# Mean and variance of h on ScalarE instead of VectorE, one iteration later

## The chip, the cores and the metric

The kernel runs on one core of a Trainium2 chip. A core has five engines with a queue each: TensorE (PE in the profile, its weight loads PEld), VectorE (DVE), ScalarE (ACT), GpSimd (POOL) and SyncE (SP), which here issues DMAs. The metric is the device time of one execution in microseconds.

## The reference

x is one sequence of 2048 tokens by 512 channels, in float32.

```python
x = A_x
h = x + A(layernorm(x))      # linear attention, 32 heads of 16
h2 = h + B(layernorm(h))     # token-mixing MLP, 2048 -> 1792 -> 2048
# A: q, k, v = x @ wqkv; phi = [softmax(p), softmax(-p)] of p = q @ w_phi (k likewise)
#    o = phi_q (phi_k^T v) / (phi_q . sum phi_k + 1e-6);  o @ wo
# B: layernorm again, u = gelu(h^T w1 + b1), y = (u w2 + b2)^T
```

`_layernorm` subtracts the mean over the 512 channels and divides by sqrt(variance + 1e-5). B applies it twice in a row, so the kernel computes one rstd that stands for both: (var·(1 + eps) + eps²)^(−1/2).

## The kernel before

Tokens lie on partitions, 16 tiles of 128 tokens. Matmuls in float32 are done as three passes over operands that are split in two parts: ScalarE rounds a value (`split`, line 56), and VectorE or GpSimd subtracts the rounded part from it (line 57).

The first stage (to about 146 us in the trace) makes keys, values and the attention state, and the queries of the first tiles. The last stage (from about 280 us) applies the rest of W1, the gelu and W2. Between them is the fused loop, `for it in range(NT + 3)`, in which the change lies. Each tile passes through it over several iterations. In iteration `it`:

- `s_num(it-1)`: TensorE makes the numerator in the PSUM tile `tn` (L544), ScalarE copies it rounded to `oh` (L548). `s_ol` later has VectorE subtract `oh` from `tn` into `ol` (L553).
- `s_wo(it-2)`: TensorE multiplies by wo into `po` (L61 to L63).
- `s_tr(it)`: TensorE transposes the scaled feature maps into `tn` (L526), ScalarE copies them to `pht` (L528). `tn` has one buffer, so the transposes wait until `ol` has read it.
- `lead(it)`: on GpSimd `s_pq(it+1)` multiplies a tile's 128x1024 feature map by its factors w (L452, called pq in the text) and `s_ez(it+3)` multiplies another by zB (L434), then the negation of logits (L159); on TensorE and ScalarE the query projections and exponentials that are still to do.
- `s_den(it+2)` and `q_sums`, `q_logits` on VectorE, ending in w (L449).
- `s_hn(it-3)`: ScalarE normalizes h into `hn` (L583) and rounds it to `hs` (L56), GpSimd subtracts for the low part of `hs` (L57).
- `s_h(it-2)`: VectorE adds `po` to x (L568), which gives h; SP writes it out; VectorE takes mean and variance (L571 to L575).
- `s_rstd(it-3)`, at the top of the iteration: GpSimd raises to the power −1/2 (L578) and multiplies the negated mean by it (L579).
- `fill`: TensorE accumulates the first two pairs of W1's column blocks with the tiles that are normalized already. `fill_load`, at the end of an iteration, brings 256 KB of W1, has ScalarE round it (`whi`, L56) and VectorE subtract (`wlo`, L57). By its condition, both pairs load at the ends of iterations 2, 6, 8, 10, 12, 14 and 16, and one pair each at the ends of 4 and 5.

The loop is written under `manual_schedule`, so TensorE, VectorE, ScalarE and GpSimd take its instructions in the order of the program. The last stage is ordered by the planner, which may place some of its instructions between the last ones of the loop; its first W2 load (L730) uses memory that the loop's last tiles occupy. In the trace, iteration n begins its copy `pht` at 147.23 (0), 155.65, 162.89, 170.30, 178.53, 187.04, 196.50, 204.36, 211.53 (8), 218.69, 225.84 (10), 232.99, and so on in steps of 7.15 to 261.61 (15).

Of the kernel before, what the change touches and what calls it, by code (L numbers as in the profile page):

```python
# [9 lines left out]
F32 = mybir.dt.float32  # L10
F32R = mybir.dt.float32r
AF = mybir.ActivationFunctionType
ALU = mybir.AluOpType
# [4 lines left out]
P = 128  # L18
S, D, H, DH, F = 2048, 512, 32, 16, 1792
NT = S // P  # L20
# [9 lines left out]
EPS = 1e-5  # L30
# [3 lines left out]
def block_kernel(ctx: ExitStack, tc: tile.TileContext, x, xT, wT, phic, wo, w1, b1, w2, b2,  # L34
                 kvmask, ident_in, out):
    nc = tc.nc

    cst = ctx.enter_context(tc.tile_pool(name="cst", bufs=1))
# [6 lines left out]
    b1s = cst.tile([P, NF], F32, name="b1s")  # L45
    b2s = cst.tile([P, NT], F32, name="b2s")
    r1 = cst.tile([P, NT], F32, name="r1")
    mv2 = cst.tile([P, NT, 2], F32, name="mv2")
    r2 = cst.tile([P, NT], F32, name="r2")
    cst.tile([P, 56], F32, name="pad")  # L50
    nc.vector.memset(ones, 1.0)
    nc.vector.memset(mhalf, -0.5)

    def split(hi, lo, src, lo_engine):

        nc.scalar.activation(hi, src, AF.Copy)  # L56
        lo_engine.tensor_sub(lo, src, hi)  # L57
# [97 lines left out]
    def negate():  # L155

        if MN:
            ev, mn = MN.pop(0)
            nc.gpsimd.tensor_sub(ev[:, :, 1], mn.unsqueeze(3).to_broadcast([P, NPR, 2, DH]), ev[:, :, 1])  # L159

    def run(*lists):

        for i in range(max(map(len, lists))):
            for ops in lists:
                if i < len(ops):
                    ops[i]()
# [4 lines left out]
    def heads(e):  # L171
        return e.rearrange("p g (a d) -> p (g a) d", d=DH)
# [186 lines left out]
    def q_mm():  # L359
        if q["mm"] < NT:  # L360
            PS[q["mm"]] = proj(q["mm"], wqh, wql, ps_q, "pu")
            q["mm"] += 1

    def q_logits(lag):
        n = q["logits"]
        if n < min(NT, q["mm"] - lag + NT * (q["mm"] == NT)):
            EQ[n] = big.tile([P, NG, P], F32, name="eq", tag="big")
            q["logits"] += 1
            return logit_ops(PS[n], EQ[n], n >= len(Q_AT))
        return []  # L370

    def q_exp(lag):
        n = q["exp"]
        if n < min(NT, q["logits"] - len(MN) - lag):
            exps(n, EQ[n])
            q["exp"] += 1

    def q_sums(lag):
        n = q["sum"]
        if n < min(NT, q["exp"] - lag + NT * (q["exp"] == NT)):  # L380
            q["sum"] += 1
            return q_sum(n)
        return []
# [48 lines left out]
    def s_ez(t):  # L432
        EZ[t] = az.tile([P, NG, P], F32, name="ez")
        nc.gpsimd.tensor_mul(EZ[t], EQ[t], zB)  # L434

    def s_den(t):


        tz = az.tile([P, NPR, 2, 2], F32, name="tz")
        den = az.tile([P, NPR, 2], F32, name="den")  # L440
        W[t] = az.tile([P, NPR, 2, 2], F32, name="w", bufs=3)
        other = SQ[t]
        return [lambda: nc.vector.reduce_sum(tz.rearrange("p g c h -> p (g c h)"), heads(EZ[t]), axis=AX.X),
                lambda: nc.vector.scalar_tensor_tensor(tz[:, :, 0], other[:, :, 1], 1e-6, tz[:, :, 0],
                                                       op0=ALU.mult, op1=ALU.add),
                lambda: nc.vector.tensor_mul(tz, other, tz),
                lambda: nc.vector.reduce_sum(den, tz.rearrange("p g c h -> p g h c"), axis=AX.X),
                lambda: nc.vector.reciprocal(den, den),
                lambda: nc.vector.tensor_mul(W[t], other, den.unsqueeze(2).to_broadcast([P, NPR, 2, 2]))]  # L449

    def s_pq(t):
        nc.gpsimd.tensor_mul(heads(EQ[t]), heads(EQ[t]), W[t].rearrange("p g c h -> p (g c h)").unsqueeze(2).to_broadcast([P, 2 * H, DH]))  # L452

    def lead(it, mm):

        if 0 <= it + 1 < NT:
            s_pq(it + 1)
        if 0 <= it + 3 < NT:
            s_ez(it + 3)
        negate()  # L460
        for _ in range(mm):
            q_mm()
        q_exp(0)
# [53 lines left out]
    ak = a2.enter_context(tc.tile_pool(name="ak", bufs=2, reuse_waits="tile"))  # L517
    ps_t = a2.enter_context(tc.tile_pool(name="ps_t", bufs=1, space=PSUM, reuse_waits="tile"))
    ps_o = a2.enter_context(tc.tile_pool(name="ps_o", bufs=1, space=PSUM, reuse_waits="tile"))
    HN, HT, PHT, OS, PO, VE = {}, {}, {}, {}, {}, {}  # L520

    def s_tr(t):
        PHT[t] = ak.tile([P, NG, P], F32, name="pht")
        ptr = ps_t.tile([P, 2, 4, P], F32, name="tn")
        for g in range(NG):
            nc.tensor.transpose(ptr[:, g // 4, g % 4, :], EQ[t][:, g, :], ident)  # L526
        for half in range(2):
            nc.scalar.activation(PHT[t][:, half * 4:half * 4 + 4, :], ptr[:, half], AF.Copy)  # L528

    def s_kv():  # L530

        pt = ps_o.tile([P, 2, P], F32, name="po")
        for b in range(2):
            nc.tensor.transpose(pt[:, b, :], kvS[:, 2 * b:2 * b + 2, :].rearrange("p n f -> p (n f)"), ident)
        nc.scalar.activation(kvB, pt, AF.Copy)

    def s_num(t):

        pn = ps_t.tile([P, 2, 4, P], F32, name="tn")[:, :, 0:2]
        for b in range(2):  # L540
            for c in range(4):
                for r in range(2):
                    rows, cols = slice(64 * r, 64 * r + 64), slice(32 * c, 32 * c + 32)
                    nc.tensor.matmul(pn[cols, r, b, :], kvB[rows, b, cols], PHT[t][rows, 4 * b + c, :],  # L544
                                     start=True, stop=True, skip_group_check=True)
        oh = ak.tile([P, 2, 2, P], F32R, name="oh")
        ol = ak.tile([P, 2, 2, P], F32R, name="ol")
        nc.scalar.activation(oh, pn, AF.Copy)  # L548
        OS[t] = oh, ol, pn

    def s_ol(t):
        oh, ol, pn = OS[t]
        return [lambda: nc.vector.tensor_sub(ol, pn, oh)]  # L553

    def s_wo(t):
        oh, ol, _ = OS.pop(t)
        PO[t] = po = ps_o.tile([P, D], F32, name="po")
        for j in range(4):
            mm3(po, oh[:, j // 2, j % 2, :], ol[:, j // 2, j % 2, :], woh[:, j, :], wol[:, j, :], j == 0, j == 3)

    def s_x(t):
        HT[t] = ak.tile([P, D], F32, name="h", bufs=4)
        nc.sync.dma_start(HT[t], x[t * P:(t + 1) * P, :])

    def s_h(t):

        h = HT[t]
        nc.vector.tensor_add(h, PO.pop(t), h)  # L568
        nc.sync.dma_start(out[t * P:(t + 1) * P, :], h)
        st = ak.tile([P, 6], F32, name="st2")  # L570
        nc.vector.bn_stats(st, h)  # L571
        nc.vector.bn_aggr(mv2[:, t, :], st)
        VE[t] = ak.tile([P, 2], F32, name="ve2")
        nc.vector.tensor_scalar(VE[t][:, 0:1], mv2[:, t, 1:2], 1.0 + EPS, EPS * EPS, op0=ALU.mult, op1=ALU.add)
        nc.vector.tensor_scalar_mul(VE[t][:, 1:2], mv2[:, t, 0:1], -1.0)  # L575

    def s_rstd(t):
        nc.gpsimd.tensor_tensor(r2[:, t:t + 1], VE[t][:, 0:1], mhalf[:, :1], op=ALU.pow)  # L578
        nc.gpsimd.tensor_mul(VE[t][:, 1:2], VE[t][:, 1:2], r2[:, t:t + 1])  # L579

    def s_hn(t):
        hn = ak.tile([P, D], F32, name="hn")
        nc.scalar.activation(hn, HT[t], AF.Identity, scale=r2[:, t:t + 1], bias=VE[t][:, 1:2])  # L583
        HN[t] = big.tile([P, 2, D], F32R, name="hs", tag="big")
        split(HN[t][:, 0], HN[t][:, 1], hn, nc.gpsimd)
# [34 lines left out]
    for it in range(NT + 3):  # L620
        if 0 <= it < NT:
            s_x(it)
        if 0 <= it - 3 < NT:
            s_rstd(it - 3)
        if 0 <= it - 1 < NT:
            s_num(it - 1)
        if 0 <= it - 2 < NT:
            s_wo(it - 2)
        if it == 1:
            q_mm()  # L630
        if 0 <= it < NT:
            s_tr(it)
        if it == 0:
            s_kv()
        lead(it, 1)
        den = s_den(it + 2) if it + 2 < NT else []
        run((s_ol(it - 1) if 0 <= it - 1 < NT else []) + q_logits(1) + (q_sums(0) if it > 0 else []), den)
        if it == 0:
            run(q_logits(0))
        if it > 0:  # L640
            negate()
        if 0 <= it - 3 < NT:
            s_hn(it - 3)
        if 0 <= it - 2 < NT:
            s_h(it - 2)
        if FN[0] <= it - LAG:
            fill(0, ps_f)
        for _ in range(2):
            if q["logits"] == NT and FN[1] <= it - LAG:
                fill(1, ps_q)  # L650
        for p in range(2):
            if it >= LAG - 2 and FL[p] <= FN[p] + 1:
                fill_load(p)
# [102 lines left out]
    for n, (sp, p) in enumerate(STEPS):  # L756
        t = 2 * sp
# [15 lines left out]
        if not last:  # L773
# [6 lines left out]
            for i, add in enumerate((u3.unsqueeze(1).to_broadcast([P, 2, HD]), e)):  # L780
                nc.vector.scalar_tensor_tensor(ot[:, i], bank[2 + i], b2s[:, t + i:t + i + 1], add,  # L781
                                               op0=ALU.add, op1=ALU.add)
# [68 lines left out]
```

## Time and profile before

| what | before |
|---|---|
| median of 3 runs | 540.12 us (540.0 to 540.82) |
| profiled execution's own time | 540.13 us |
| span of the profile | 538.3 us |
| PE busy | 526.6 us, 98% |
| DVE busy | 393.3 us, 73% |
| ACT busy | 257.9 us, 48% |
| POOL busy | 235.6 us, 44% |

The span runs from the first to the last instruction; the own time is a little longer. Shares are means over stages that differ. In a timeline row stand the start and the duration in us, the engine, the line of the kernel, the operation, what it writes and reads, the shapes, how many like instructions are merged, and in brackets the idle time of the engine before it and what ended that.

### The profile page before, as it was taken

To read this page: it belongs to the slowest core of one execution; us is meant where nothing else is said; L and a number is where in the kernel's file an instruction comes from. 1 tells how busy PE (TensorE), PEld (TensorE's weight loads), DVE (VectorE), ACT (ScalarE), POOL (GpSimd) and SP (SyncE) were. 2 spreads that over 40 slices of the span, in tenths; PEclk is the share of its full clock that TensorE was granted. 3 is DMA by queue.
4 is the path that set the end of the run, shared out by engine and by line. 5 is a ranking of instruction groups with operands and counts; after the bars stand their busy time and mean duration, and the time that the engine had idled before them with its cause. 6 is when DMAs were issued, how large, how long until landed. Compare 5 with 4: busy or idle time off the path is not lost.

```text
span 538.3 us, 9897 instructions
## 1 busy us (share of the span) xinstructions
PE 526.6 (98%) x3872; PEld 449.7 (84%) x3872; DVE 393.3 (73%) x722; ACT 257.9 (48%) x406; POOL 235.6 (44%) x184
## 2 busy tenths in 40 slices
PE   8999999999999999999999999999999999999995
PEld 7888778777776877787787888888899999999995
DVE  6992999974689989996447952224858878977784
ACT  6998733525346465444647433325552333343340
POOL 2589599788968979996432200000001101101110
PEclk9999999999999999999999999999999999999999
DMA  8633201012301233333254543333013565645631
GB/s 310 207 102 117 79 21 40 1 62 78 93 6 63 95 99 94 107 131 119 82 163 143 163 139 97 99 97 99 20 40 100 140 153 129 126 138 119 157 71 48
DMA packets 45486, 55.84 MB, mean 104 GB/s; under 512 B 3968, under 2 KB 33024, under 8 KB 45440
## 3 DMA queue, kind: packets, MB, share of 16 engines
q1 hardware_dynamic: 43136, 51.38, 30.1%
q0 software_dynamic: 2016, 3.67, 5.0%
q8 instruction: 30, 0.49, 0.4%
q10 hardware_dynamic: 288, 0.17, 0.1%
q14 instruction: 16, 0.13, 0.1%
HBM read 46.81 MB, written 8.39 MB: 103 GB/s over the span
## 4 chain that ended last, share of the span: by engine, by line
PE 85%; DVE 8%; ACT 2%; DMA 2%; issue 2%; POOL 0%; SPq 0%; DVEq 0%; POOLq 0%; ACTq 0%
PE py L745 26%; PE pu L61 10%; PE pu L63 10%; PE pu L62 10%; PE po L61 3%; PE pk_ps L61 3%; PE pv L62 3%; PE pv L61 3%; PE pv L63 3%; PE pk_ps L62 2%; PE pk_ps L63 2%; PE po L62 2%; PE po L63 2%; PE tn L526 2%; PE kvp L205 2%
## 5 line engine op out<-in xcount | busy, mean ns | idle before, releaser
L57 DVE TENSOR_TENSOR wlo<-wraw,whi 128x512 fp32r<-128x512 f32 (+1 forms) x84 | 99.4, 1195 | 66.8 <-ACT whi L56 66.5
L56 ACT ACTIVATE whi<-wraw 128x512 fp32r<-128x512 f32 (+1 forms) x84 | 81.9, 986 | 128.7 <-PE py L745 73.8
L783 POOL DMA_DIRECT2D out<-ot x14 | 12.5, 1000 | 206.0 <-DVE ot L781 206.0
L745 PE MATMUL py<-uf,whi 128*128 128x256 f32 x560 | 96.2, 283 | 0.0
L61 PE MATMUL pu<-hs,whi 128*128 128x512 f32 x224 | 87.6, 394 | 0.6 <-ACT eq L146 0.6
L62 PE MATMUL pu<-hs,whi 128*128 128x512 f32 x224 | 87.2, 389 | 0.0
L63 PE MATMUL pu<-hs,wlo 128*128 128x512 f32 x224 | 86.3, 391 | 0.7 <-DVE wlo L57 0.7
L745 PEld LDWEIGHTS py<-uf,whi 128*128 128x128 f32 x560 | 83.3, 192 | 0.0
L745 PE MATMUL py<-uf,wlo 128*128 128x256 f32 x280 | 69.9, 283 | 0.0
L63 PEld LDWEIGHTS pu<-hs,wlo 128*128 128x128 f32 x224 | 41.7, 188 | 10.6 <-DVE wlo L57 2.1
L61 PEld LDWEIGHTS pu<-hs,whi 128*128 128x128 f32 x224 | 42.1, 188 | 9.5 <-ACT eq L146 1.1
L745 PEld LDWEIGHTS py<-uf,wlo 128*128 128x128 f32 x280 | 49.7, 192 | 0.0
L62 PEld LDWEIGHTS pu<-hs,whi 128*128 128x128 f32 x224 | 42.1, 188 | 8.3
L528 ACT ACTIVATE pht<-tn 128x512 f32<-128x512 f32 x32 | 17.4, 596 | 50.4 <-PE tn L526 50.4
L434 POOL TENSOR_TENSOR ez<-eq,zB 128x1024 f32<-128x1024 f32 x16 | 38.4, 2400 | 0.7 <-ACT zB L488 0.7
L745 PE MATMUL py<-un,whi 128*128 128x256 f32 x224 | 38.4, 283 | 0.0
L193 POOL TENSOR_TENSOR pk<-pk,sk 128x1024 f32<-128x1024 f32 x16 | 31.1, 1946 | 9.7 <-DVE sk L192 5.4
L745 PEld LDWEIGHTS py<-un,whi 128*128 128x128 f32 x224 | 33.2, 192 | 0.1
L452 POOL TENSOR_TENSOR eq<-eq,w 128x1024 f32<-128x1024 f32 x16 | 31.0, 1939 | 4.4 <-DVE w L449 4.4
L197 POOL TENSOR_TENSOR zacc<-zacc,pk 128x1024 f32<-128x1024 f32 x13 | 31.4, 2412 | 0.4
L57 POOL TENSOR_TENSOR hs<-hn,hs 128x512 fp32r<-128x512 f32 x16 | 20.6, 1290 | 21.2 <-ACT hs L56 21.2
L61 PE MATMUL po<-woh,oh 128*128 128x512 f32 x64 | 26.6, 416 | 1.0 <-DVE h L568 1.0
(161 smaller groups left out, 1146.3 us busy)
## 6 DMA issues: line engine op xcount, KB each, us to landing
wraw<-in_w SPq DMA_DIRECT2D x112, 256.0 KB, 2.9
xraw<-in_xT SPq DMA_DIRECT2D x16, 256.0 KB, 3.1
xh<-in_x SPq DMA_DIRECT2D x16, 256.0 KB, 2.6
h<-in_x SPq DMA_DIRECT2D x16, 256.0 KB, 3.0
out<-h SPq DMA_DIRECT2D x16, 256.0 KB, 2.4
out<-ot POOLq DMA_DIRECT2D x14, 256.0 KB, 4.3
wraw<-in_wT SPq DMA_DIRECT2D x12, 256.0 KB, 5.1
wo<-in_wo SPq DMA_DIRECT2D x4, 256.0 KB, 4.7
```

The source lines that it names most:

```text
L56: nc.scalar.activation(hi, src, AF.Copy)
L57: lo_engine.tensor_sub(lo, src, hi)
L61: nc.tensor.matmul(o, ah, bh, start=first, stop=False)
L62: nc.tensor.matmul(o, ah, bl, start=False, stop=False)
L63: nc.tensor.matmul(o, al, bh, start=False, stop=last)
L193: nc.gpsimd.tensor_mul(heads(PK[t]), heads(PK[t]), sk.unsqueeze(2).to_broadcast([P, 2 * H, DH]))
L197: nc.gpsimd.tensor_add(zacc, zacc, PK[t])
L434: nc.gpsimd.tensor_mul(EZ[t], EQ[t], zB)
L452: nc.gpsimd.tensor_mul(heads(EQ[t]), heads(EQ[t]), W[t].rearrange("p g c h -> p (g c h)").unsqueeze(2).to_broadcast([P, 2 * H, DH]))
L528: nc.scalar.activation(PHT[t][:, half * 4:half * 4 + 4, :], ptr[:, half], AF.Copy)
L745: nc.tensor.matmul(o, a[x], b[:, y], start=start and i == 0, stop=stop and i == 2, skip_group_check=True)
L783: nc.gpsimd.dma_start(out[(t + i) * P:(t + i + 1) * P, :], flat(ot[:, i]), accum_op=ALU.add)
```

## The change

The four statistics instructions of VectorE go. In their place ScalarE makes two passes with an accumulated sum over h: a Copy scaled by −1/512 gives the negated mean, a Square with that as bias gives the sum of squared deviations; an Identity on one column turns it into var·(1 + eps) + eps². These stand behind the copy `oh` of the iteration after the one in which h is made. `s_pq` moves from `lead` to a place ahead of it, and `s_rstd` from the top of the iteration to behind `s_pq`, so GpSimd's order is now pq, power and product, ez. `ve2` has three buffers instead of two, a scratch tile of 512 columns is new, and the padding in the constants' pool is widened.

```diff
-    mv2 = cst.tile([P, NT, 2], F32, name="mv2")
+    eps2 = cst.tile([P, 1], F32, name="eps2")
     r2 = cst.tile([P, NT], F32, name="r2")
-    cst.tile([P, 56], F32, name="pad")
+    cst.tile([P, 80], F32, name="pad")
     nc.vector.memset(ones, 1.0)
     nc.vector.memset(mhalf, -0.5)
+    nc.vector.memset(eps2, EPS * EPS)
...
     def lead(it, mm):
-        if 0 <= it + 1 < NT:
-            s_pq(it + 1)
         if 0 <= it + 3 < NT:
             s_ez(it + 3)
...
         nc.vector.tensor_add(h, PO.pop(t), h)
         nc.sync.dma_start(out[t * P:(t + 1) * P, :], h)
-        st = ak.tile([P, 6], F32, name="st2")
-        nc.vector.bn_stats(st, h)
-        nc.vector.bn_aggr(mv2[:, t, :], st)
-        VE[t] = ak.tile([P, 2], F32, name="ve2")
-        nc.vector.tensor_scalar(VE[t][:, 0:1], mv2[:, t, 1:2], 1.0 + EPS, EPS * EPS, op0=ALU.mult, op1=ALU.add)
-        nc.vector.tensor_scalar_mul(VE[t][:, 1:2], mv2[:, t, 0:1], -1.0)
+
+    def s_moments(t):
+
+        VE[t] = ak.tile([P, 2], F32, name="ve2", bufs=3)
+        junk = ak.tile([P, D], F32, name="hj", bufs=1)
+        var = ak.tile([P, 1], F32, name="hv")
+        nc.scalar.activation(junk, HT[t], AF.Copy, scale=-1.0 / D, accum_out=VE[t][:, 1:2])
+        nc.scalar.activation(junk, HT[t], AF.Square, bias=VE[t][:, 1:2], accum_out=var)
+        nc.scalar.activation(VE[t][:, 0:1], var, AF.Identity, scale=(1.0 + EPS) / D, bias=eps2)
...
     for it in range(NT + 3):
         if 0 <= it < NT:
             s_x(it)
-        if 0 <= it - 3 < NT:
-            s_rstd(it - 3)
         if 0 <= it - 1 < NT:
             s_num(it - 1)
+        if 0 <= it - 3 < NT:
+            s_moments(it - 3)
         if 0 <= it - 2 < NT:
             s_wo(it - 2)
...
         if it == 0:
             s_kv()
+        if 0 <= it + 1 < NT:
+            s_pq(it + 1)
+        if 0 <= it - 3 < NT:
+            s_rstd(it - 3)
         lead(it, 1)
```

## The prediction

> **What bounds the kernel now.** I read the page's head first, then one iteration of the fused loop by the windows, then its timeline engine by engine.
>
> ```profile
> span 538.3 us, 9897 instructions
> PE 526.6 (98%) x3872; PEld 449.7 (84%) x3872; DVE 393.3 (73%) x722; ACT 257.9 (48%) x406; POOL 235.6 (44%) x184
> ...
> 225.84:232.99 7.15, 7.15 (x65) 5.65 (x64) 6.91 (x15) 3.97 (x7) 6.67 (x6) 1.00 0.43 140
> ```
>
> TensorE is busy for 98% of the span, at full granted clock (1.00) in the window. Only its gaps can be won, and only new gaps can cost. In the window, which is one steady iteration (first transpose copy to first transpose copy), TensorE is full, but VectorE has 6.91 and GpSimd 6.67 of the 7.15 us: neither has room for a wait that TensorE would not notice. The order in which these two meet is the point to read.
>
> ```profile
> 227.95 0.69 DVE L571 BATCH_NORM_STATS2 st<-h 128x6 f32<-128x512 f32 x1
> 228.20 1.14 ACT L56 ACTIVATE whi<-wraw 128x512 fp32r<-128x512 f32 x2
> 228.37 1.28 POOL L57 TENSOR_TENSOR hs<-hn,hs 128x512 fp32r<-128x512 f32 x1 [0.40 <-ACT hs L56]
> 228.72 0.62 ACT L56 ACTIVATE whi<-wraw 128x512 fp32r<-128x512 f32 x1
> 229.03 1.17 DVE L57 TENSOR_TENSOR wlo<-wraw,whi 128x512 fp32r<-128x512 f32 x1
> 229.24 0.60 ACT L548 ACTIVATE oh<-tn 128x512 fp32r<-128x512 f32 x1
> 229.61 1.00 POOL L578 TENSOR_TENSOR r<-ve,mhalf 128x1 f32<-128x1 f32 x1
> 230.12 0.68 DVE L57 TENSOR_TENSOR wlo<-wraw,whi 128x512 fp32r<-128x512 f32 x1
> 230.73 0.68 DVE L553 TENSOR_TENSOR ol<-tn,oh 128x512 fp32r<-128x512 f32 x1
> 230.83 1.94 POOL L452 TENSOR_TENSOR eq<-eq,w 128x1024 f32<-128x1024 f32 x1
> 231.92 0.38 PE L526 MATMUL tn<-ident,eq 128*128 128x128 f32 x2
> 232.99 1.09 ACT L528 ACTIVATE pht<-tn 128x512 f32<-128x512 f32 x2 [3.15 <-PE tn L526]
> ```
>
> These rows are the end of iteration 10 and the start of 11. Two streamed pieces of W1 are split: ScalarE rounds (whi), VectorE subtracts (wlo). The first subtraction takes 1.17 us, the second 0.68. The first ran while GpSimd was in its own 512-column subtraction (hs, 228.37 to 229.65) and ended 0.55 after that at 230.20; the second ran beside the power for rstd, one column wide, and was not slowed. Behind them VectorE makes ol (230.73 to 231.41), which must have read tn before TensorE may transpose into it at 231.92. That leaves TensorE 0.51 us, some 0.15 of which is the hand-over (the next fence has it without slack). So a second wlo that is late by more than about 0.36 stops TensorE.
>
> Does GpSimd's long multiplication (L452, here pq) slow VectorE as its subtraction does? Its twin in form, L193, shows it:
>
> ```profile
> 25.99 1.94 POOL L193 TENSOR_TENSOR pk<-pk,sk 128x1024 f32<-128x1024 f32 x1 [0.16 <-DVE sk L192]
> 26.68 1.53 DVE L256 TENSOR_SCALAR wraw<-wraw,mu 128x512 f32<-128x512 f32 x1
> ...
> 287.06 0.96 DVE L736 TENSOR_TENSOR wraw<-wraw 128x256 f32<-128x256 f32 x1
> 287.82 0.80 POOL L693 TENSOR_TENSOR tt<-u,tt 128x256 f32<-128x256 f32 x1
> 287.94 0.96 DVE L734 TENSOR_TENSOR wraw<-wraw 128x256 f32<-128x256 f32 x1
> ...
> 202.43 0.68 DVE L553 TENSOR_TENSOR ol<-tn,oh 128x512 fp32r<-128x512 f32 x1
> 203.26 0.41 PE L526 MATMUL tn<-ident,eq 128*128 128x128 f32 x2 [0.52 <-DVE ol L553]
> ...
> 216.57 0.68 DVE L553 TENSOR_TENSOR ol<-tn,oh 128x512 fp32r<-128x512 f32 x1
> 217.62 0.93 PE L526 MATMUL tn<-ident,eq 128*128 128x128 f32 x7
> ...
> 245.03 0.68 DVE L553 TENSOR_TENSOR ol<-tn,oh 128x512 fp32r<-128x512 f32 x1
> 246.23 1.03 PE L526 MATMUL tn<-ident,eq 128*128 128x128 f32 x8
> ```
>
> The 1.53 us operation ends at 28.21, 0.28 after the multiplication's end at 27.93: it waited for all of it. And the two engines take turns: L693 came at 287.82 while L736 ran (to 288.02) and went next; L734, issued at 287.94, ended at 288.90, 0.28 after L693. Operations that read PSUM (ol at 230.73 beside L452) keep 0.68.
>
> The Trainium skill (SBUF — State Buffer, section "SBUF: two separate sides") calls this pair of ports an exclusive lock: whoever starts first has it for the whole instruction, the other fully blocks. By that rule a blocked wlo would run its whole 0.68 after the release where the trace shows 0.55, 0.13 more in each of the five pairs below, and the time would be 549.3; the trace's number decides.
>
> **The change, part by part.** VectorE loses four instructions a tile: 229.03 − 227.95 = 1.08 us, of which nothing lies on the path where TensorE is full. In iteration 10 VectorE would come to the first wlo at 227.95, but whi is ready only at 228.20 + 0.63 = 228.83, and hs holds the port until 229.65: the first wlo ends at 230.20, as before.
>
> GpSimd's order changes. Power and product (L578, L579) move behind pq (L452), so pq stands directly behind hs, where the short power was. Its factor w is an iteration old and ready. pq asks at 229.61, before the second wlo is issued at 230.12, so by the turns above it goes at 230.20 and holds for 1.90, to 232.10. The second wlo ends 0.55 later at 232.65, not at 230.80: 1.85 late. ol follows and ends at 233.26, and TensorE transposes at 233.41 instead of 231.92: +1.5. This repeats wherever two pieces are split at the end of an iteration and the next one has a pq: the ends of 2, 6, 8, 10 and 12. (4 and 5 split one piece each; 15 has no pq.) Each costs 1.85 less the slack between ol's end plus 0.15 and the transpose:
> - into 7: 203.11 to 203.26 is all hand-over: +1.85
> - into 9: 217.25 to 217.62, slack 0.22: +1.6
> - into 11: +1.5
> - into 13: 245.71 to 246.23, slack 0.37: +1.5
>
> Sum 6.45. They don't absorb one another: the engines behind the transpose shift with it.
>
> The end of iteration 2 is the one place where VectorE binds:
>
> ```profile
> 165.38 1.16 ACT L56 ACTIVATE whi<-wraw 128x512 fp32r<-128x512 f32 x2
> 165.57 1.06 POOL L159 TENSOR_TENSOR eq<-mn,eq 128x512 f32<-128x512 f32 x1 [0.77 <-ACT eq L146]
> 168.31 0.68 DVE L553 TENSOR_TENSOR ol<-tn,oh 128x512 fp32r<-128x512 f32 x1
> 169.14 0.95 PE L526 MATMUL tn<-ident,eq 128*128 128x128 f32 x7
> 173.85 0.68 DVE L568 TENSOR_TENSOR h<-po,h 128x512 f32<-128x512 f32 x1
> 174.59 0.50 PE L61 MATMUL po<-woh,oh 128*128 128x512 f32 x1 [1.03 <-DVE h L568]
> ```
>
> From ol to h VectorE works without a break (5.54 us), and TensorE's 1.03 us wait at 174.59 is for h. Without the statistics the first wlo starts when whi is there, at 166.01, but now beside the negation (165.57 to 166.63): it ends at 167.18. pq holds to 169.08, the second wlo ends at 169.63, ol starts at 169.56 instead of 168.31, and h and TensorE's product come 1.25 later: +1.25. If the negation, of which no row shows a block, held nothing, this would be +0.8; without any block −1.05, the statistics' worth.
>
> ScalarE gains the passes:
>
> ```profile
> 63.99 0.62 ACT L112 ACTIVATE sqj<-xh 128x512 f32<-128x512 f32 x1
> 65.46 1.14 ACT L169 ACTIVATE eq<-eq,r 128x1024 f32<-128x1024 f32 x1
> ```
>
> The same two passes with their accumulator reads took 65.46 − 63.99 = 1.47 us. The one-column Identity has no row: between nothing and the 0.62 of a pass; I take 0.3, as it has one column. The Trainium skill (ScalarE: Activation LUTs, "What ACT_TABLE_LOAD costs") gives about 0.28 us for it as an estimate, which would leave the sum as it is. 1.8 us in all, behind oh (next start 229.76), done by 231.55; ScalarE is idle until 232.99. Cost nothing in the loop; without that 3.15 us wait they would delay pht by up to 1.8. rstd then follows pq without waiting. The added memset at the start lies under the first loads: nothing.
>
> At the end no transposes cover the passes:
>
> ```profile
> 273.32 0.69 DVE L568 TENSOR_TENSOR h<-po,h 128x512 f32<-128x512 f32 x1 [2.27 <-PE po L63]
> 275.30 1.04 POOL L578 TENSOR_TENSOR r<-ve,mhalf 128x1 f32<-128x1 f32 x1 [1.27 <-DVE ve L575]
> 275.82 0.63 ACT L56 ACTIVATE whi<-wraw 128x512 fp32r<-128x512 f32 x1 [0.73 <-PE pu L62]
> 278.20 1.29 POOL L57 TENSOR_TENSOR hs<-hn,hs 128x512 fp32r<-128x512 f32 x1 [1.59 <-ACT hs L56]
> 279.52 0.88 SPq L730 DMA_DIRECT2D wraw<-in_w  x2
> 294.23 0.30 PEld L63 LDWEIGHTS pu<-hs,wlo 128*128 128x128 f32 x2 [1.07 <-DVE wlo L57]
> ```
>
> From h's end (274.01) to the power was 1.29 us; with the passes it is 1.8: +0.5 if ScalarE is free. The chain of the tile before grows by the same and may still hold ScalarE with its own hn and hs; I add 0.3 for that. The last hs releases the buffers of the first W2 load on SP's queue (279.52), and what VectorE does with that load stands ahead of a wlo for which TensorE already waits at 294.23. I take +0.8, between 0 (the next wait swallows it) and +2.9 (the passes queue behind the whi copy that ends at 276.45, 2.4 after h, and take their 0.5 more).
>
> Sum: 1.25 + 6.45 + 0.8 = +8.5. Against the profiled execution's own 540.13 us (span 538.3; median of the runs 540.12, the same): **548.6 us**.
>
> **The rivals.**
> A. VectorE keeps the port from one wlo to the next, so pq waits instead. Then no transpose is late; at the end of 2 the second wlo ends at 167.8, ol starts 0.6 earlier, and 0.6 is won at 174.59: 540.13 − 0.6 + 0.8 = 540.3, no change; with no block by GpSimd at all 540.13 − 1.05 + 0.5 = 539.6, and 539.1 with the end hidden. What decides is who goes at 230.20. For it: nothing in the rows; against it: L693 before L734. The Trainium skill (Perfetto Trace Analysis, "Optimizing Scalar/DVE Operations") says that offloading a saturated VectorE to ScalarE may make sense; by it the 1.05 would come. Chance 0.13.
> B. The passes bind: pq and rstd are late, the end costs its 2.9 and each wlo its whole 0.68: 548.6 + 2.1 + 0.65 = 551.3. For it: VectorE and GpSimd have little room; against it: 3.15 us of idle ScalarE. Chance 0.07.
> C. Only part of the pairs collide, because hs and pq drift as GpSimd is delayed: two or three of the five, about 544. For it: GpSimd must run hs on time for the pattern to repeat; against it: hs waits for ScalarE (0.40 at 228.37), not for GpSimd. Chance 0.08.
>
> **How the numbers follow.** The forecast has 0.72 with its own range 546.5 to 551. 542 to 551 leaves out A and what lies above, under 2 in 10. 0.2% is 1.1 us, about what can be told from no change: A splits into 0.09 same and 0.04 faster; all else is slower, 0.87.
>
> **What would show it.** Right: in the profile after, second wlo's of about 2.5 us beside L452, L452's mean above 1939 ns, transposes waiting for ol into 3, 7, 9, 11 and 13, ScalarE's passes between oh and pht, the statistics gone from VectorE. Wrong: second wlo's at 0.68 with L452 stretched instead (A); pht late behind the passes (B).

## The result and the profile after

The changed kernel takes 549.11 us (median of 5 runs, 548.19 to 549.4) against 540.0 of the kernel before on the same chip (539.88 to 540.82): ratio 1.0164, 95% interval 1.015 to 1.0178. It is slower by 9.1 us, where 548.6 was forecast. Two later sets gave 549.79 (ratio 1.0168, 1.0153 to 1.0184) and 549.0 (1.0158, 1.0139 to 1.0178).

The profiled execution took 548.19 us, 8.06 more than that of before. In the changed kernel's profile, the lines up to the loop have numbers one higher (L57 is now L58, L452 is L453), `s_ol` is L552, the transposes L525, the power L580 and its product L581, the passes L575 to L577. From the head of its page, the chain's shares and the costliest group:

```profile
span 546.4 us, 9894 instructions
PE 527.4 (97%) x3872; PEld 449.5 (82%) x3872; DVE 387.9 (71%) x659; ACT 285.2 (52%) x486; POOL 236.4 (43%) x184
...
PE 78%; DVE 7%; POOL 5%; ACT 4%; DMA 2%; issue 2%; SPq 0%; DVEq 0%; POOLq 0%; ACTq 0%
...
L58 DVE TENSOR_TENSOR wlo<-wraw,whi 128x512 fp32r<-128x512 f32 (+1 forms) x84 | 110.1, 1321 | 81.3 <-ACT whi L57 81.1
```

TensorE's busy time is almost unchanged (526.6 before), so most of the 8 us are new gaps. VectorE lost 64 tile-statistics instructions, but its busy time fell by only 5.4 us, because the split subtractions took 10.7 us more (99.4 before): the time in which an instruction is blocked counts as busy. GpSimd now holds 5% of the chain that ended last, where it held 0% before.

The same stretch as in the prediction, the end of iteration 10 and the start of 11, from the timeline of after:

```profile
233.06 1.28 POOL L58 TENSOR_TENSOR hs<-hn,hs 128x512 fp32r<-128x512 f32 x1 [0.68 <-ACT hs L57]
233.54 1.35 DVE L58 TENSOR_TENSOR wlo<-wraw,whi 128x512 fp32r<-128x512 f32 x1 [1.02 <-ACT whi L57]
234.31 2.38 POOL L453 TENSOR_TENSOR eq<-eq,w 128x1024 f32<-128x1024 f32 x1
234.82 2.42 DVE L58 TENSOR_TENSOR wlo<-wraw,whi 128x512 fp32r<-128x512 f32 x1
236.65 0.99 POOL L580 TENSOR_TENSOR r<-ve,mhalf 128x1 f32<-128x1 f32 x1
237.16 0.68 DVE L552 TENSOR_TENSOR ol<-tn,oh 128x512 fp32r<-128x512 f32 x1
237.72 0.19 POOL L581 TENSOR_TENSOR ve<-ve,r 128x1 f32<-128x1 f32 x1
237.99 0.63 PE L525 MATMUL tn<-ident,eq 128*128 128x128 f32 x4 [1.21 <-POOL ve L581]
```

The turns are all here. hs ends at 234.34 and the first wlo 0.55 later. pq, issued at 234.31, goes next and ends at 236.69, 0.44 longer than its usual 1.94 because it waited for that wlo. The second wlo, issued at 234.82, ends at 237.24, again 0.55 after GpSimd's end: 2.42 us instead of 0.68. ol ends at 237.84 and TensorE goes on at 237.99.

The last row is put down to the product of GpSimd (ve, L581), and so are all five late transposes in the waits of after (7.3 us in 5 waits, the longest 2.3):

```profile
PE tn L525 <- POOL ve L581: 7.3, 5, 2.3
```

The product, L581, ran from 237.72 to 237.91, and ol ended at 237.84; the two ended within 0.07 us of each other, and the profile names whichever came last. But the transposes read a feature map and write `tn`; the product is made from the statistics of an older tile and is no operand of theirs. In the iteration before, 9 to 10, the transposes begin 0.39 us ahead of that iteration's product, so they can't be waiting for it there:

```profile
229.46 1.04 PE L525 MATMUL tn<-ident,eq 128*128 128x128 f32 x8
...
229.85 0.19 POOL L581 TENSOR_TENSOR ve<-ve,r 128x1 f32<-128x1 f32 x1
```

The releaser's name is no proof, and the experiments below decide.

The other places: end of iteration 2 into 3, and end of 6 into 7.

```profile
165.73 1.06 POOL L160 TENSOR_TENSOR eq<-mn,eq 128x512 f32<-128x512 f32 x1 [0.78 <-ACT eq L147]
166.20 1.14 DVE L58 TENSOR_TENSOR wlo<-wraw,whi 128x512 fp32r<-128x512 f32 x1
166.75 2.39 POOL L453 TENSOR_TENSOR eq<-eq,w 128x1024 f32<-128x1024 f32 x1
167.27 2.42 DVE L58 TENSOR_TENSOR wlo<-wraw,whi 128x512 fp32r<-128x512 f32 x1
169.61 0.68 DVE L552 TENSOR_TENSOR ol<-tn,oh 128x512 fp32r<-128x512 f32 x1
...
203.19 2.42 DVE L58 TENSOR_TENSOR wlo<-wraw,whi 128x512 fp32r<-128x512 f32 x1
205.53 0.68 DVE L552 TENSOR_TENSOR ol<-tn,oh 128x512 fp32r<-128x512 f32 x1
206.35 1.06 PE L525 MATMUL tn<-ident,eq 128*128 128x128 f32 x8 [2.27 <-POOL ve L581]
```

Measured from the start of one iteration's transposes to the next (first rows of L526 and L525 in the timelines), the iterations that grew are these:

| from, to | before | after | grew | forecast |
|---|---|---|---|---|
| 2 to 3 | 7.39 | 8.53 | 1.14 | 1.25 |
| 6 to 7 | 7.83 | 9.57 | 1.74 | 1.85 |
| 8 to 9 | 7.16 | 8.67 | 1.51 | 1.6 |
| 10 to 11 | 7.15 | 8.53 | 1.38 | 1.5 |
| 12 to 13 | 7.15 | 8.54 | 1.39 | 1.5 |
| sum | | | 7.16 | 7.7 |

Every other iteration is within 0.08 us of before. The sum and these small differences make 7.43 from the transposes of 0 to those of 15.

ScalarE's passes, in iteration 14 to 15 of after:

```profile
265.44 0.60 ACT L547 ACTIVATE oh<-tn 128x512 fp32r<-128x512 f32 x1
265.93 0.62 ACT L575 ACTIVATE hj<-h 128x512 f32<-128x512 f32 x1
266.46 0.19 ACT L575 ACTIVATION_READ_ACCUMULATOR hj<-h 128x1 f32 x1
266.68 0.73 ACT L576 ACTIVATE hj<-h,ve 128x512 f32<-128x512 f32 x1
267.31 0.19 ACT L576 ACTIVATION_READ_ACCUMULATOR hj<-h,ve 128x1 f32 x1
267.53 0.30 ACT L577 ACTIVATE ve<-hv,eps 128x1 f32<-128x1 f32 x1
269.19 1.09 ACT L527 ACTIVATE pht<-tn 128x512 f32<-128x512 f32 x2 [1.36 <-PE tn L525]
```

They take 1.90 us, done at 267.83, and ScalarE still waits 1.36 us for TensorE before pht.

### The profile page after: what moved, and what is told of

The parts are those of the page before. It is cut to its first block, busy times and chain, and to the rows that moved or that the text cites. A ratio compares the mean times of both kernels' runs of the same rounds, so it can differ in the third digit from the quotient of the medians.

```text
span 546.4 us, 9894 instructions
## 1 busy us (share of the span) xinstructions
PE 527.4 (97%) x3872; PEld 449.5 (82%) x3872; DVE 387.9 (71%) x659; ACT 285.2 (52%) x486; POOL 236.4 (43%) x184
## 4 chain that ended last, share of the span: by engine, by line
PE 78%; DVE 7%; POOL 5%; ACT 4%; DMA 2%; issue 2%; SPq 0%; DVEq 0%; POOLq 0%; ACTq 0%
PE py L751 25%; PE pu L62 9%; PE pu L64 9%; PE pu L63 9%; PE pk_ps L62 3%; PE pv L63 3%; PE pv L62 3%; PE pv L64 2%; PE pk_ps L63 2%; PE pk_ps L64 2%; PE tn L525 2%; POOL eq L453 2%; PE po L62 2%; PE kvp L206 2%; PE po L64 2%; PE po L63 2%
## 5 line engine op out<-in xcount | busy, mean ns | idle before, releaser
L58 DVE TENSOR_TENSOR wlo<-wraw,whi 128x512 fp32r<-128x512 f32 (+1 forms) x84 | 110.1, 1321 | 81.3 <-ACT whi L57 81.1
L57 ACT ACTIVATE whi<-wraw 128x512 fp32r<-128x512 f32 (+1 forms) x84 | 82.0, 987 | 124.8 <-PE py L751 71.1
L453 POOL TENSOR_TENSOR eq<-eq,w 128x1024 f32<-128x1024 f32 x16 | 34.2, 2139 | 4.4 <-DVE w L450 4.4
L58 POOL TENSOR_TENSOR hs<-hn,hs 128x512 fp32r<-128x512 f32 x16 | 20.6, 1288 | 24.5 <-ACT hs L57 24.5
L170 ACT ACTIVATE pk<-pk,r 128x1024 f32<-128x1024 f32 x16 | 18.4, 1150 | 18.3 <-DVE pk L150 18.3
```

Of the source, the lines that this page charges most:

```text
L170: nc.scalar.activation(e, e, AF.Exp, scale=r1[:, t:t + 1])
```

## The experiments

The ratios are against runs of the kernel before on the same chip (540.45 us for the first four, 540.67 for the next three and the repetition of the changed kernel, 540.47 for the last ones).

**GpSimd's order alone.** The kernel before, statistics still on VectorE, with pq and rstd moved as the change moves them:

```diff
     def lead(it, mm):
-        if 0 <= it + 1 < NT:
-            s_pq(it + 1)
...
-        if 0 <= it - 3 < NT:
-            s_rstd(it - 3)
         if 0 <= it - 1 < NT:
             s_num(it - 1)
...
             s_kv()
+        if 0 <= it + 1 < NT:
+            s_pq(it + 1)
+        if 0 <= it - 3 < NT:
+            s_rstd(it - 3)
         lead(it, 1)
```

> The kernel before with GpSimd's new order alone: pq ahead of power and product; the statistics stay on VectorE, and ScalarE has no passes. Theory (pq behind hs blocks the second wlo of a pair): the transposes into 7, 9, 11 and 13 are late by 1.7, 1.5, 1.4 and 1.4 us as in the changed kernel, that into 3 by about 1.2; +7.2 us, about 547.2. Rival (ScalarE's passes and the later rstd cost the time): no change, 540.0.

Measured: 549.53 us (549.34 to 550.19), ratio 1.0164 (1.015 to 1.0179), the whole of the change's cost without its passes. The five iterations grew by 7.14 us in sum, where they grew by 7.16 in the changed kernel. The rival (no change) is out. The size missed by 2.3 us. Of the profiled execution's 549.34, one stretch accounts for 1.6; two of its windows, and then rows of TensorE there:

```profile
204.00:208.00 4.00, 1.74 (x12) 1.34 (x11) 4.00 (x4) 0.02 (x1) 3.92 (x4) 0.99 0.36 94
208.00:212.00 4.00, 4.00 (x12) 3.02 (x11) 3.73 (x10) 3.44 (x5) 1.59 (x2) 0.59 0.15 52
```

```profile
206.88 1.06 PE L524 MATMUL tn<-ident,eq 128*128 128x128 f32 x8 [2.26 <-POOL ve L577]
...
209.81 0.63 PE L63 MATMUL pu<-hs,wlo 128*128 128x512 f32 x1
...
211.65 0.39 PE L62 MATMUL pu<-hs,whi 128*128 128x512 f32 x1
```

The last three figures of a window are the granted clock, the DMA share and the rate: 0.59 in 208 to 212, that is half clock for 3.3 of the 4 us. Narrower windows put the whole stretch at 207.9 to 211.3, 3.4 us, behind the 2.26 us wait into iteration 7. Matmuls take 0.63 instead of 0.39 us, and that iteration lasts 8.79 instead of 7.2. The loop also began 0.6 later (146.68 against 146.10). What is left, 547.2, is what the theory gave.

**The split subtraction out of pq's way.** The changed kernel, in which VectorE's part of a split is kept back and issued behind `tz` of the next iteration, beside the power (in iteration 3, behind h):

```diff
-        split(wh_, wl_, raw, nc.vector)
+        if late:
+            nc.scalar.activation(wh_, raw, AF.Copy)
+            LO.append(lambda: nc.vector.tensor_sub(wl_, raw, wh_))
...
+        run(ops[:1], den[:1])
+        if it != 3:
+            lows()
+        run(ops[1:], den[1:])
```

> The changed kernel, with the wlo subtractions of the loop moved on VectorE from ahead of ol to behind tz of the next iteration (in iteration 3 behind h), where GpSimd does the short power. Passes and GpSimd's order stay. Theory: no wlo stands beside pq, all five waits go, and with them those of before at 169.14, 174.59 and 203.26 (0.2 + 1.0 + 0.7); what is left is the end, +0.7: about 538.8. Rival (the passes cost): about 547 to 549.

Measured: 540.64 us (540.05 to 541.72), ratio 1.0002 (0.9991 to 1.0013). All five waits are gone (from the transposes of 2, 6, 8, 10 and 12 to the next is 7.15 or 7.16 us), with GpSimd's new order and the passes still there. GpSimd's product too still stands behind pq: in iteration 7 it begins at 204.51, and the transposes had begun at 202.64, without it. Of the 1.8 us over the expectation, some 1.5 are where the moved work stands in front of h or ol:

```profile
203.34 1.28 DVE L600 TENSOR_TENSOR wlo<-wraw,whi 128x512 fp32r<-128x512 f32 x2
...
207.26 0.68 DVE L567 TENSOR_TENSOR h<-po,h 128x512 f32<-128x512 f32 x1
...
208.00 0.50 PE L62 MATMUL po<-woh,oh 128*128 128x512 f32 x1 [0.99 <-DVE h L567]
```

A pair now takes 1.28 us, two times 0.68 overlapped, but it stands ahead of h, and TensorE's product by wo waits 0.99 us. The iteration whose transposes begin at 177.42, where ol stood behind the pair of iteration 2, is 0.5 us longer than with the better places below (7.83 and 7.31).

**pq in two halves.** The changed kernel with pq as two instructions of 512 columns:

```diff
-        nc.gpsimd.tensor_mul(heads(EQ[t]), heads(EQ[t]), ...)
+        for i in range(2):
+            e = heads(EQ[t])[:, i * H:(i + 1) * H]
+            nc.gpsimd.tensor_mul(e, e, ...)
```

> The changed kernel with pq as two instructions of 512 columns each. Theory (a blocked wlo waits for the one GpSimd instruction that is ahead of it, and the engines take turns): the second wlo is 0.9 late instead of 1.85; the transposes into 7, 9, 11, 13 cost 0.9, 0.65, 0.5, 0.5 instead of 6.0 in all and that into 3 0.3 instead of 1.2: 4.4 us less, about 544.7. Rival within the theory (the port is shared, or GpSimd holds it over both halves): 549. Rival (passes): 549.

Measured: 544.16 us (543.91 to 545.13), ratio 1.0067 (1.0049 to 1.0085). The second wlo now goes between the halves:

```profile
200.97 2.84 DVE L58 TENSOR_TENSOR wlo<-wraw,whi 128x512 fp32r<-128x512 f32 x2 [2.04 <-ACT whi L57]
201.74 2.99 POOL L456 TENSOR_TENSOR eq<-eq,w 128x512 f32<-128x512 f32 x2
```

The pair takes 2.84 us in place of the 3.7 or so of the changed kernel. The five late transposes still wait, 0.32 to 1.39 us, and the profile now puts all five down to ol. The cost follows the length of the one GpSimd instruction that is waited for, as turns at a port say and a general shortage of VectorE does not.

**The kernel before with its subtractions moved.** Is there something to win without the change? The pairs loaded at the ends of 2 and 6 go behind h, GpSimd's order and the statistics as before:

```diff
+        if it not in (3, 7):
+            lows()
+        run(ops, den)
...
             s_h(it - 2)
+        lows()
```

> The kernel before, with only the two pairs of wlo that stand ahead of a late transpose (those loaded at the ends of 2 and 6) moved behind h of the next iteration. Theory: the waits at 169.14, 174.59 and 203.26 go (0.2 + 1.0 + 0.7): about 538.1. If it is as fast as the changed kernel with its wlo moved, the passes on ScalarE bring nothing by themselves. Rival (VectorE's statistics are what binds there): 539.5 to 540.

Measured: 540.74 us (540.26 to 541.52), ratio 1.0002 (0.9993 to 1.001). A miss: the waits only moved, to ol of the next iteration.

```profile
175.11 2.05 DVE L598 TENSOR_TENSOR wlo<-wraw,whi 128x512 fp32r<-128x512 f32 x2
177.09 0.68 DVE L553 TENSOR_TENSOR ol<-tn,oh 128x512 fp32r<-128x512 f32 x1
...
177.91 0.52 PE L526 MATMUL tn<-ident,eq 128*128 128x128 f32 x3 [0.84 <-DVE ol L553]
```

**Better places.** The changed kernel, with the pair of 2 behind `tz` of iteration 4, one of the pair of 6 behind h of 7 and the other behind `tz` of 8, and the statistics of tiles 13 to 15 on VectorE:

```diff
-        if it != 3:
+        if it not in (3, 7):
             lows()
...
             s_h(it - 2)
-        lows()
+        if it == 7:
+            lows(1)
```

> The changed kernel with wlo moved behind tz, but the pair loaded at the end of 2 waits until behind tz of iteration 4, of the pair loaded at the end of 6 one goes behind h of 7 and one behind tz of 8, and tiles 13 to 15 have their statistics on VectorE again. Theory: against the version with wlo moved (540.6) the waits for ol into 4 (0.5) and for h in 8 (1.2) go, and the end's 0.7: about 538.2, 2.2 below before. Rival (time is lost elsewhere when VectorE's order changes): 540 to 541.

Measured: 539.71 us (539.03 to 540.25), ratio 0.9984 (0.9975 to 0.9993). That is 0.16% below the kernel before, less than was expected, and in the repetition below the interval reaches no difference. TensorE's waits for h of 0.92 and 0.23 us remain, at 182.81 and 214.03.

**The same places in the order of before.** Pair of 2 behind `tz` of 4, pair of 6 behind `tz` of 8:

```diff
+        if it not in (3, 4, 7, 8):
+            lows()
+        run(ops[:1], den[:1])
+        if it in (4, 8):
+            lows()
+        run(ops[1:], den[1:])
```

> The kernel before, statistics on VectorE, GpSimd's order unchanged, with the pair of wlo loaded at the end of 2 moved behind tz of iteration 4 and that of 6 behind tz of 8; the later pairs stay ahead of ol. Theory: the waits at 169.14, 174.59 and 203.26 go (1.9), the second pair's wlo meets pq and h of 8 is late by about 0.6: about 539.1. If it is as fast as the one with the passes, these bring nothing.

Measured: 548.92 us (548.09 to 549.42), ratio 1.0156 (1.0142 to 1.017). A miss of 9.8 us, and the most telling one:

```profile
176.04 1.94 POOL L452 TENSOR_TENSOR eq<-eq,w 128x1024 f32<-128x1024 f32 x1
176.19 5.15 DVE L598 TENSOR_TENSOR wlo<-wraw,whi 128x512 fp32r<-128x512 f32 x2
177.94 2.85 POOL L434 TENSOR_TENSOR ez<-eq,zB 128x1024 f32<-128x1024 f32 x1
```

```profile
PE po L61 <- DVE h L568: 5.4, 2, 3.9
```

```profile
185.00:189.00 4.00, 3.19 (x8) 2.52 (x9) 3.90 (x9) 1.36 (x3) 3.36 (x5) 0.50 0.46 147
189.00:193.00 4.00, 4.00 (x17) 3.30 (x16) 3.96 (x11) 0.48 (x1) 3.45 (x2) 0.65 0.16 51
```

These are its timeline, a row of its waits, and two of its windows. In the order of before GpSimd runs pq and ez at that place. Each wlo waits for one of them: 5.15 us for a pair that takes 1.28 beside the power. h comes late, TensorE waits up to 3.9 us for it (until 185.81), and its clock stands at half for 6.8 us from 185.0 on (4 us at 0.50, 2.8 of the next 4). That iteration, 4 to 5, lasts 14.89 us instead of 8.52. The pair of 6 meets pq and ez in the same way behind `tz` of 8 (5.03 us), and 8 to 9 lasts 11.24 instead of 7.16. The expectation had considered what VectorE does at the new place, not what GpSimd does.

**The statistics of the last three tiles back on VectorE**, in the changed kernel:

```diff
+        if t >= 13:
+            st = ak.tile([P, 6], F32, name="st2")
...
+            nc.vector.bn_stats(st, h)
...
+        if t >= 13:
+            return
```

> The changed kernel with the statistics of tiles 13 to 15 on VectorE again; the loop as changed. Theory (the passes cost 0.8 at the end, where nothing covers them): 0.7 to 0.8 below the changed kernel run beside it. Rival (the end is hidden): the same as it.

Measured: 548.28 us (547.52 to 549.18), against 549.79 (548.3 to 550.12) of the changed kernel on the same chip.

> The changed kernel on the chip of the other three, to compare them: 549.1. Where its profile shows TensorE at a lower granted clock behind the 2.4 us idle ahead of the transpose into 7, the iteration behind it is about 1.6 longer, as in the run with GpSimd's order alone.

The profile of this repetition, one of the short executions, shows full clock behind the wait into 7, so the second half of its expectation was not put to the test. The medians differ by more than expected, the profiled executions by less: spans of 546.2 and 546.5. With the statistics back on VectorE the last hs ends 2.9 us earlier (286.62, 289.50), but the first product with W2 comes 131.56 us behind the transposes of 15, against 131.72 in the repetition and 131.59 in the first profile of the changed kernel. So the passes at the end cost at most 0.2 us there; the rest of the difference in medians is not explained by it.

**Are the passes worth anything?** The version with better places once more, and beside it the same with all statistics on VectorE (`t >= 0` for `t >= 13`), that is, with no passes at all:

> The placed version again (GpSimd's new order, every second subtraction kept clear of pq), but with the statistics of all tiles on VectorE as before and no passes on ScalarE. Theory: the passes bring nothing by themselves where TensorE is full, so the time is that of the placed version, 539.7 us, within 0.5. Rival: what the placed version won over before comes from VectorE's 1.08 us a tile being free; then this one falls back to 540.3 or above, with new waits of TensorE for ol or h near 170, 175 and 214 us.

> The placed version once more on the same chip as the one with all statistics on VectorE: 539.7 us (539.0 to 540.3).

Measured: 542.84 us (542.28 to 543.27), ratio 1.0042 (1.003 to 1.0055), against 540.06 (539.59 to 540.63), ratio 0.9992 (0.9984 to 1.0001). My theory missed: without the passes it is 2.8 us slower, 3.2 in the profiles. One iteration has half of that, 6 to 7 (8.77 instead of 7.15). In it, first without the passes, then with:

```profile
194.37 0.55 POOL L590 TENSOR_TENSOR r<-ve,mhalf 128x1 f32<-128x1 f32 x1
195.14 2.38 POOL L435 TENSOR_TENSOR ez<-eq,zB 128x1024 f32<-128x1024 f32 x1
195.24 2.83 DVE L610 TENSOR_TENSOR wlo<-wraw,whi 128x512 fp32r<-128x512 f32 x1
200.70 0.68 DVE L567 TENSOR_TENSOR h<-po,h 128x512 f32<-128x512 f32 x1
```

```profile
195.13 0.68 DVE L610 TENSOR_TENSOR wlo<-wraw,whi 128x512 fp32r<-128x512 f32 x1
195.23 0.99 POOL L590 TENSOR_TENSOR r<-ve,mhalf 128x1 f32<-128x1 f32 x1 [0.94 <-ACT ve L587]
196.44 2.41 POOL L435 TENSOR_TENSOR ez<-eq,zB 128x1024 f32<-128x1024 f32 x1
198.45 0.68 DVE L567 TENSOR_TENSOR h<-po,h 128x512 f32<-128x512 f32 x1
```

With the statistics made early the power runs at once, ez follows and comes 0.1 us ahead of the wlo, which waits for all of it; h is late, and TensorE waits 1.50 us for it at 201.44. With the passes the power waits 0.94 us for ScalarE, and by that ez comes behind the wlo. So the rival's time came out for another reason than the rival's in this iteration: not VectorE's free time, but which of the two asks first. 0.4 us more went in the next iterations, in waits for h of 0.55 us at 216.38 and 0.25 at 223.86 (0.24 at 214.36 with the passes), and 1.1 behind the loop, of which TensorE's waits for wlo make 0.4 (1.08 us in three, 0.65 in one with the passes). What causes these is open, and the rival may hold for them.

**The changed kernel a third time**, for its longer executions:

> The changed kernel once more: 548.2 to 550.1 us. If a stretch of half clock behind one of its 2.4 us waits is what separates its longer executions from the profiled one, a profile above 549 shows such a stretch, some 3.4 us long and worth about 1.6; if not, such a profile shows the clock at 1.00 through the loop.

Measured: 549.0 us (548.09 to 550.4); the profiled execution was again a short one, 548.17, with all clocks of the loop at 1.00. So the test did not come about. In the 13 executions of the changed kernel, the profiled ones were among the shortest (548.17 to 548.3, mean granted clock 0.997); seven of the other ten show 0.994 or 0.995, as the execution with the half-clock stretch above does (0.995), and these are 549.11 to 550.4. That fits such a stretch of 1.6 us in them, but no profile of one was taken, so it is not shown.

## Why the prediction was right

**GpSimd's order and the turns: right.** The place and the rule came out at every one of the five ends, and the sizes within 0.12 us. pq goes between two wlo and the second ends 0.55 us after it. That the order alone costs the whole, that moving the wlo away takes it back, and that halving pq takes back a part of the size that was expected, shows that this is the cause, against the profile's own label on the waits.

**The five sizes: all 0.09 to 0.12 too high**, 7.16 for 7.7. In iteration 10 to 11 the step "ends at 232.65, 1.85 late" was 2.42 − 0.68 = 1.74 late: the step let pq hold the port for 1.90 from the first wlo's end, and in after pq ended 1.80 after it (234.89 to 236.69). The Trainium skill (SBUF — State Buffer, section "SBUF: two separate sides") says that the instruction that comes second fully blocks, which the prediction took to mean a whole 0.68 us after the release. The runs don't agree in that size: it is 0.55 us in all rows above. That the second instruction waits for all of the first, they do show.

**The negation at the end of iteration 2: right.** The step that had no row, that the 1.06 us negation holds the port, shows in after: the first wlo there (166.20 to 167.34) ends 0.55 after the negation (166.79).

**Passes in the loop at no cost: right.** 1.90 us for 1.8 estimated, 0.30 for the one-column Identity, under a wait of 3.15 that is now 1.36 and nowhere in the loop shorter.

**The end, +0.8: right in sign, half in size, and not by the step named.** From the transposes of 15 (260.54 and 268.12) to the first product with W2 it is 131.10 and 131.59 us, +0.49:

```profile
391.64 0.28 PE L745 MATMUL py<-un,whi 128*128 128x256 f32 x1
```

```profile
399.71 0.28 PE L751 MATMUL py<-un,whi 128*128 128x256 f32 x1
```

What was wrong is the step by which the late last hs carries through to TensorE. It did come late (2.46 us more behind the transposes), as in the case for the upper bound, but the run with the statistics of the last tiles back on VectorE has it 2.9 us earlier and gains at most 0.2, so almost all of it is hidden. The 0.49 is about what TensorE's waits for wlo behind the loop grew: 0.40 us at 303.94 and 0.79 at 313.44 in after, 0.65 at 294.23 in before. Why they fall otherwise is open.

**The sum.** Profile to profile +8.06 for +8.5 (0.15 ahead of the loop, 7.43 in it, 0.49 behind it). The median is 0.9 us above the profiled execution, which the prediction had not allowed for. The two misses have opposite signs, so that the median, 549.11, came within 0.5 of 548.6 is in part luck.

**Rivals.** A, that VectorE keeps the port from one wlo to the next, is refuted by the rows of all five ends. B, that the passes bind, by pht's 1.36 us wait for TensorE and by the order alone, which costs the same without passes. C, that only part of the pairs collide, by the table. That the removed statistics gain nothing where TensorE is full held for this kernel (7.14 us lost at the five ends with them, 7.16 without). What the 1.08 us a tile free of VectorE may be worth with another order, the comparison without passes does not separate from who comes first.

## What to carry to other kernels

When an instruction is moved on GpSimd, or a two-operand one on VectorE, read both engines' timelines at the new place: the same 0.68 us subtraction took 2.4 us beside pq and 2.8 beside ez, and two in a row can each wait for one. Moving 1.9 us of GpSimd's work ahead by 1.2 us cost 1.6% of a kernel that keeps TensorE at 98%, while taking 1.08 us a tile off VectorE did not pay for it. A wait's label names what ended last; if that is no operand of the waiting instruction and something else ended within 0.1 us of it, move one of the two before believing the label.

## What the runs showed of the hardware

A wait of TensorE of 2.3 us can be followed by a stretch of half clock. In the run of the order alone it is 3.4 us long, worth 1.6 us, and begins 1.0 us after the 2.26 us wait has ended. In the run with the same places in the order of before it is 6.8 us long and begins within the wait of 3.9, 3.1 us after its start. It isn't certain to follow. The changed kernel has a wait as long (2.27, the row at 206.35), and the same window of its profile stands at full clock:

```profile
208.00:212.00 4.00, 4.00 (x48) 2.93 (x47) 2.97 (x8) 3.97 (x8) 1.61 (x2) 1.00 0.18 49
```

The Trainium skill (TensorE: Matmul & The Clock Gate, "Part 1: The HAM clock gate") puts the half clock behind an idle window of about 3.4 us, and the return behind as long a busy one. The stretch of 3.4 us agrees with the return, and that of 6.8 is twice as long; the idle time was shorter here, 2.26 us in one run and 3.1 in the other when the clock fell.
